# A decode attention kernel: where TensorE's loop lies in its code blocks, and how the second pair's values are loaded

## The chip, the cores and the metric

One core of a Trainium2 chip runs the whole kernel. The metric is the device time of one execution in microseconds; the time of the kernel before is the median of three runs.

## The reference

Attention for one new token: 32 query heads, 8 key/value heads (4 queries share one), 65,536 keys of 128 numbers, all bfloat16.

```
B, Hq, Hkv, Sq, Sk, D = 1, 32, 8, 1, 65536, 128
k = jnp.repeat(k, rep, axis=1); v = jnp.repeat(v, rep, axis=1)     # rep = 4
scores = jnp.einsum("bhqd,bhkd->bhqk", q, k) * D ** -0.5
p = softmax(scores, axis=-1)
return jnp.einsum("bhqk,bhkd->bhqd", p, v)
```

K and V are 134 MB each and every byte is used once, so 268 MB have to come in from memory.

## The kernel before

**Units, pairs, rounds.** The keys of a head are cut into 4 units of 128 x 128 keys; two units make a *pair*, and a *round* works on one pair. There are 16 pairs (`NR`), two for each head. A pair is 256 tiles of 128 keys, 8.39 MB of K and 8.39 MB of V. Tiles 0 to 159 (`A`) go to the first unit of an even pair and the other 96 (`C`) to the second; an odd pair is turned round by `C` tiles, so that it can lie in a ring buffer (`row_tile`).

**What each engine does in a round.** TensorE transposes K in groups of 8 tiles (`pe_transposes`, L139), VectorE and ScalarE copy each group out of PSUM (`evict`, L233 and L235), and 8 groups later TensorE multiplies the transposed tiles with the queries (`pe_scores`, L157). The first 20 groups (`GA`) are one run of code for every round; the last 12 stand in two copies, one under `If(i % 2 > 0)` and one under `If(i % 2 < 1)`, since an odd pair lies elsewhere in the K buffer. VectorE and GpSimd find the maximum, ScalarE the exponentials (L403). Then TensorE multiplies the exponentials with V (`pe_values`, L183) in three *stretches* (`stretch`): stretch 1 is tiles 96 to 159, stretch 2 is tiles 160 to 255, stretch 0 is tiles 0 to 95. Stretch 1 comes first in each round. In an even round stretch 0 follows, then stretch 2, by an inner loop of two turns whose code has stretch 2 ahead of stretch 0: the first turn jumps over stretch 2, and the second jumps back to it. An odd round makes the second turn alone, with both.

**Loops in code.** TensorE's 16 rounds are one loop in its code (`Fori` over `NR`), with some 1,750 instructions in its body. Ahead of it stands an `addr_align(256, offset=LOOP_SLOT, ...)`: the instruction that follows is placed `LOOP_SLOT` instructions behind an address that is a multiple of 256 instructions. `max_nops` is how many empty instructions may fill the room before it; beyond that, the room is jumped over.

**Buffers and transfers.** SyncE issues every load of K and V, in order, in one queue. There is one K buffer with 96 tiles to spare and a single V buffer of one pair. A K load waits for `kfree`, which ScalarE or VectorE sets when the first 20 groups of the pair before are transposed. A V load waits for `vfree`, which VectorE sets in `add_values` when TensorE has finished all stretches of the pair before (`pvd`). Pair 0 is loaded without a wait, K in three parts and V whole. Pairs 2 to 13 go through `load_both`: K whole and V whole. The last two pairs are split into parts again, so that TensorE can start on what has landed.

Pair 1 is loaded by lines of its own. When TensorE ends stretch 1 of round 0 it sets `vmid`; SyncE waits for that and loads the middle of V, tiles 96 to 159, before `vfree`. Behind `vfree` it loads tiles 160 to 255, then 0 to 95, each with a semaphore of its own (`vrdy[0]`, `vrdy[1]`, `vpiece[0]`), for which the stretches of round 1 wait one by one.

Of the kernel before, what the change touches and what calls it, by code (L numbers as in the profile page):

```python
# [13 lines left out]
T = 128  # L14
C = 96
A = 2 * T - C
# [9 lines left out]

V_PIECES = (62, 22, 9, 3)

LOOP_SLOT = 0


def on_act(j):
# [9 lines left out]
def take(e, sem, n=1):  # L42

    e.wait_ge(sem, n)
    e.sem_inc(sem, -n)  # L45


def bass_standalone__gqa_softmax__decode_kernel(nc, q, k, v, out):
# [14 lines left out]
    def row_tile(odd, x):  # L63
        return (x + C) % (2 * T) if odd else x
# [9 lines left out]
    def sem(name):  # L74
        return S(nc.semaphore(name))
# [40 lines left out]
    krdy = [sem(f"krdy{i}") for i in range(len(K_PARTS))]  # L116
    vrdy = [sem(f"vrdy{i}") for i in range(2)]
    vpiece = [sem(f"vpiece{i}") for i in range(len(V_PIECES))]
    kfree, vfree, vmid = sem("kfree"), sem("vfree"), sem("vmid")
    trd, tra, evd, eva = sem("trd"), sem("tra"), sem("evd"), sem("eva")  # L120
    qkd, qrdy, pvd = sem("qkd"), sem("qrdy"), sem("pvd")
    cm, cma, ng, exd, sx, lrd, lra = (sem(n) for n in ("cm", "cma", "ng", "exd", "sx", "lrd", "lra"))
# [41 lines left out]
    def pe_keys(pe, i):  # L164
        for j in range(GA + LAG):
            if j < GA:
                pe_transposes(pe, j, C + j * TB)
            if j >= LAG:
                pe_scores(pe, j - LAG)
        with pe.If(i % 2 > 0):  # L170
            for j in range(GA, G):
                pe_transposes(pe, j, j * TB - A)
        with pe.If(i % 2 < 1):
            for j in range(GA, G):
                pe_transposes(pe, j, C + j * TB)
        for j in range(GA, G):
            pe_scores(pe, j)

    def stretch(pe, q):
        a, b = ((0, C), (C, A), (A, 2 * T))[q]  # L180
        starts = [sum(V_PIECES[:n]) for n in range(len(V_PIECES))] if q == 0 else []
        for r in range(a, b):
            ins = pe.matmul(vsum[q], lhsT=vbuf[:, r * D:(r + 1) * D], rhs=pts[:, r * R:(r + 1) * R],  # L183
                            start=r == a, stop=r == b - 1)
            if r in starts:
                ins.wait_op(vpiece[starts.index(r)], 16, "sem-ge")
        return ins

    def pe_values(pe, i):

        take(pe, vrdy[0], 16)
        take(pe, exd)
        stretch(pe, 1).then_inc(vmid, 1)


        with pe.Fori(i % 2, 2) as s:
            with pe.If(s > 0):
                take(pe, vrdy[1], 16)  # L200
                take(pe, exd)
                stretch(pe, 2).then_inc(pvd, 1)
            with pe.If((i + s) % 2 < 1):
                take(pe, exd)
                stretch(pe, 0).then_inc(pvd, 1)

    def pe_last(pe):
        ins = pe.transpose(fin[0:R, 0:P], acc, identf[:, :])  # L208
        ins.wait_op(t_acc, 1, "sem-ge")
        ins.then_inc(s_fin, 1)  # L210

    def tensor_engine(pe):
        pe.wait_ge(q_sem, 16)
        pe.wait_ge(t_id, 1)
        pe.transpose(trb[0][:, 0:HR], qsb[:, :], ident[0:HR, 0:HR]).then_inc(s_x, 1)
        pe.wait_ge(t_qT, 1)
        pe.addr_align(256, offset=LOOP_SLOT, max_nops=16)
        with pe.Fori(0, NR) as i:
            pe_keys(pe, i)
            pe_values(pe, i)  # L220
        pe_last(pe)
# [221 lines left out]
    def pairs(x):  # L443

        return x.rearrange("h (c p t) d -> (h c) p (t d)", c=HALVES, p=P)

    def sync_engine(e):
        kp, vp = pairs(kf), pairs(vf)

        def cols(a, b):  # L450
            return slice(a * D, b * D)

        def load_k(i, odd, split=(0,)):

            for n, f in enumerate(split):
                last = (split + (len(K_PARTS),))[n + 1]
                a, b = K_PARTS[f], (K_PARTS + (2 * T,))[last]
                r = row_tile(odd, a) if b - a < 2 * T else 0
                t = r if odd else C + r
                e.dma_start(kbuf[:, cols(t, t + b - a)], kp[i][:, cols(r, r + b - a)]).then_inc(krdy[f], 16)  # L460
                for x in range(f + 1, last):
                    e.sem_inc(krdy[x], 16)

        def load_v(i, ready, a, b):
            e.dma_start(vbuf[:, cols(a, b)], vp[i][:, cols(a, b)]).then_inc(ready, 16)

        def load_both(i, odd):
            take(e, kfree)
            load_k(i, odd)
            take(e, vfree)  # L470
            load_v(i, vrdy[0], 0, 2 * T)
            e.sem_inc(vrdy[1], 16)

        load_k(0, 0, (0, 1, 2))
        load_v(0, vrdy[0], 0, 2 * T)

        for sm in [vrdy[1]] + vpiece:
            e.sem_inc(sm, 16)

        take(e, kfree)  # L480
        load_k(1, 1)
        e.wait_ge(vmid, 1)
        load_v(1, vrdy[0], C, A)
        take(e, vfree)
        e.sem_inc(vpiece[0], -16)
        load_v(1, vrdy[1], A, 2 * T)
        load_v(1, vpiece[0], 0, C)
        with e.Fori(1, H - 1) as h:
            load_both(2 * h, 0)
            load_both(2 * h + 1, 1)  # L490
        i = NR - 2
        take(e, kfree)
        load_k(i, 0, (0, 2))
        take(e, vfree)
        load_v(i, vrdy[0], 0, A)
        load_v(i, vrdy[1], A, 2 * T)
        i = NR - 1
        take(e, kfree)
        load_k(i, 1, (0, 1, 2))
        take(e, vfree)  # L500
        for sm in vpiece:
            e.sem_inc(sm, -16)
        load_v(i, vrdy[0], C, 2 * T)
        e.sem_inc(vrdy[1], 16)
        r = 0
        for n, sm in zip(V_PIECES, vpiece):
            load_v(i, sm, r, r + n)
            r += n
        ins = e.dma_start(of[HR - R:HR, :], olast[:, :])
        ins.wait_op(t_last, 1, "sem-ge")  # L510
        ins.then_inc(o_sem, 16)

    with nc.Block() as block:
        block.tensor(tensor_engine)
        block.vector(vector_engine)
        block.scalar(scalar_engine)
        block.gpsimd(gpsimd_engine)
        block.sync(sync_engine)
# [30 lines left out]
```

## Time and profile before

| | |
|---|---|
| median of three runs | 628.77 us (628.72 to 628.85) |
| the profiled execution: its time, its span | 628.62 us, 627.1 us |
| TensorE: multiplies busy, weight loads busy | 490.4 us (78%), 485.9 us (77%) |
| VectorE, ScalarE, GpSimd busy | 284.5 us (45%), 235.4 us (38%), 16.5 us (3%) |
| read from memory | 268.44 MB, 428 GB/s over the span |
| mean granted clock of TensorE | 0.769 |

The span is the time from the first to the last instruction of the profiled execution; 1.5 us of its time lie around it. TensorE's busy time counts pipelined instructions from end to end and follows the granted clock, so it is not a measure of how close it is to its limit. "Queue q1" in the profile is the queue in which SyncE's loads stand; q8 and q14 bring in code. A time to landing is counted from the issue of a transfer to the moment its semaphore is set, and so holds the time for which it stood behind others.

### The profile page before, as it was taken

What the parts mean: (1) busy time and instruction counts of PE and PEld (TensorE: products, weight loads), DVE (VectorE), ACT (ScalarE), POOL (GpSimd) and SP (SyncE); (2) the same over time, 40 slices, a digit from 0 to 9 for tenths busy, and PEclk for the clock granted to TensorE, in tenths of its full rate; (3) what the DMA queues carried; (4) which work ended last, traced back from release to release, by engine and by line L of the source; (5) the groups of instructions that cost most, each with busy time, mean ns of one, the idle gap of its engine ahead of it and who ended that gap; (6) DMA issues with size and microseconds to landing.
All of it is one profiled execution on the core that took longest, in us unless ns stands there. A gap on an engine that the chain in (4) does not pass through costs nothing. (4 is left out here: it accounts for less than half of the span.)

```text
span 627.1 us, 26947 instructions
## 1 busy us (share of the span) xinstructions
PE 490.4 (78%) x12290; PEld 485.9 (77%) x12290; DVE 284.5 (45%) x667; ACT 235.4 (38%) x466; POOL 16.5 (3%) x49
## 2 busy tenths in 40 slices
PE   4664995949959497696976949779595896999887
PEld 3664995949959497696976949779495896989887
DVE  4340553615536164351644516345172452747364
ACT  2240442504425053251533605335052351535343
POOL 0000000000000000000000000000000000000000
PEclk9875886958869597685977959779596785969696
DMA  9999999999999999999999999999999999999997
GB/s 375 430 450 403 442 450 435 435 435 431 422 443 426 435 435 426 439 431 431 435 431 439 431 439 431 435 435 435 435 435 435 435 435 431 412 432 426 432 438 306
DMA packets 6443, 268.59 MB, mean 428 GB/s; under 512 B 802, under 2 KB 930, under 8 KB 1186
## 3 DMA queue, kind: packets, MB, share of 16 engines
q1 hardware_dynamic: 6344, 268.44, 99.2%
q8 instruction: 7, 0.11, 0.1%
q10 hardware_dynamic: 90, 0.02, 0.0%
q14 instruction: 2, 0.02, 0.0%
HBM read 268.44 MB, written 0.01 MB: 428 GB/s over the span
## 5 line engine op out<-in xcount | busy, mean ns | idle before, releaser
L139 PE MATMUL trb<-ident,kbuf 128*128 128x128 bf16 x4096 | 303.4, 237 | 107.4 <-PEq L45 101.7
L139 PEld LDWEIGHTS trb<-ident,kbuf 128*128 128x128 bf16 x4096 | 271.1, 107 | 109.1 <-issue 108.8
L233 ACT ACTIVATE ktb<-trb 128x1024 bf16<-128x1024 bf16 x176 | 180.2, 1024 | 349.9 <-PE trb L139 343.5
L235 DVE COPY ktb<-trb 128x1024 bf16<-128x1024 bf16 x336 | 221.8, 689 | 170.2 <-PE trb L139 167.2
L157 PE MATMUL qkb<-qcur,ktb 128*128 128x4 bf16 x4096 | 132.3, 164 | 1.0 <-issue 1.0
L157 PEld LDWEIGHTS qkb<-qcur,ktb 128*128 128x128 bf16 x4096 | 124.5, 96 | 1.1 <-issue 1.1
L183 PE MATMUL pvb<-pts,vbuf 128*128 128x4 bf16 x2560 | 71.6, 165 | 13.8 <-PEq L45 9.9
L183 PEld LDWEIGHTS pvb<-pts,vbuf 128*128 128x128 bf16 x2560 | 69.8, 101 | 15.6 <-issue 15.2
L403 ACT ACTIVATE pts<-qkb,negm 128x160 bf16<-128x160 f32 (+1 forms) x128 | 52.0, 548 | 0.0
L183 PE MATMUL qkb<-pts,vbuf 128*128 128x4 bf16 x1536 | 43.4, 166 | 7.7 <-PEq L45 7.7
L270 DVE TENSOR_REDUCE cmax<-qkb 128x4 f32<-128x640 f32 (+1 forms) x32 | 22.1, 692 | 59.2 <-DVEq L45 59.2
L183 PEld LDWEIGHTS qkb<-pts,vbuf 128*128 128x128 bf16 x1536 | 42.4, 104 | 8.3 <-issue 8.2
L403 ACT ACTIVATION_READ_ACCUMULATOR pts<-qkb,negm 128x1 f32 x128 | 34.1, 267 | 0.0
L439 POOL PARTITION_ALL_REDUCE cmaxa<-cmax x32 | 12.1, 377 | 576.3 <-POOLq L45 576.3
L320 DVE COPY acc<-qkb 128x4 f32<-128x4 f32 x8 | 1.3, 162 | 41.2 <-DVEq L45 41.2
L397 ACT ACTIVATE alpha<-dm 128x4 f32<-128x4 f32 x32 | 6.4, 201 | 32.4 <-ACTq L45 32.4
L298 DVE TENSOR_TENSOR lp<-lp,alpha 128x4 f32<-128x4 f32 x24 | 3.9, 163 | 26.9 <-DVEq L45 26.9
L309 DVE TENSOR_TENSOR acc<-acc,pvb 128x4 f32<-128x4 f32 x32 | 5.1, 158 | 20.9 <-DVEq L45 20.0
L287 DVE TENSOR_TENSOR m<-m,cmaxa 128x4 f32<-128x4 f32 x24 | 3.8, 160 | 8.8 <-DVEq L45 8.8
L306 DVE TENSOR_TENSOR acc<-acc,alpha 128x4 f32<-128x4 f32 x24 | 3.9, 162 | 4.2 <-DVEq L45 3.7
L299 DVE TENSOR_TENSOR lp<-lp,rsum 128x4 f32<-128x4 f32 x24 | 3.9, 162 | 0.8
L288 DVE TENSOR_TENSOR dm<-m 128x4 f32<-128x4 f32 x24 | 3.9, 162 | 0.8
(42 smaller groups left out, 30.2 us busy)
## 6 DMA issues: line engine op xcount, KB each, us to landing
kbuf<-in_k_dram SPq DMA_DIRECT2D x5, 3072.0 KB, 24.6
vbuf<-in_v_dram SPq DMA_DIRECT2D x2, 5120.0 KB, 23.5
vbuf<-in_v_dram SPq DMA_DIRECT2D x3, 3072.0 KB, 19.9
kbuf<-in_k_dram SPq DMA_DIRECT2D x1, 5120.0 KB, 17.7
kbuf<-in_k_dram SPq DMA_DIRECT2D x2, 2048.0 KB, 12.7
vbuf<-in_v_dram SPq DMA_DIRECT2D x1, 2048.0 KB, 17.8
vbuf<-in_v_dram SPq DMA_DIRECT2D x1, 1984.0 KB, 31.3
vbuf<-in_v_dram SPq DMA_DIRECT2D x1, 704.0 KB, 32.6
```

Source lines behind the costliest of these rows:

```text
L139: ins = pe.transpose(trb[j % NTB][:, i * P:(i + 1) * P], kbuf[:, t * D:(t + 1) * D], ident[:, :])
L157: ins = pe.matmul(bank[:, t * R:(t + 1) * R], lhsT=ktb[:, off:off + P], rhs=qcur[:, :], start=True, stop=True)
L183: ins = pe.matmul(vsum[q], lhsT=vbuf[:, r * D:(r + 1) * D], rhs=pts[:, r * R:(r + 1) * R], start=r == a, stop=r == b - 1)
L233: ins = e.activation(dst, trb[j % NTB][:, :], AF.Copy).then_inc(eva, 1)
L235: ins = e.tensor_copy(dst, trb[j % NTB][:, :]).then_inc(evd, 1)
L270: e.tensor_reduce(cmax[:, :], qkb[part][:, 0:n * R].rearrange("p (t g) -> p g t", g=R), AX.X, ALU.max).then_inc(cm, 1)
L288: lambda: e.tensor_tensor(dm[u % 2][:, :], mo[:, :], mn[:, :], ALU.subtract),
L298: chain(e, lambda: e.tensor_tensor(lp[:, :], lp[:, :], alpha[u % 2][:, :], ALU.mult), lambda: e.tensor_tensor(lp[:, :], lp[:, :], rsum[u % ...
L309: return lambda: e.tensor_tensor(acc, acc, vsum[q], ALU.add)
L397: e.activation(alpha[u % 2][:, :], dm[u % 2][:, :], AF.Exp, scale=scale)
L403: ins = e.activation(pv[:, g, r:r + n], sv[:, g, 0:n], AF.Exp, bias=negm[b][:, g:g + 1], scale=scale, accum_out=rsum[b][:, g:g + 1])
L439: e.partition_all_reduce(cmaxa[:, :], cmax[:, :], P, bass.bass_isa.ReduceOp.max).then_inc(cma, 1)
```

## The change

The loop of TensorE begins 33 instructions behind a multiple of 256 rather than on one, and up to 64 empty instructions may stand ahead of it. The mark `vmid` is gone from TensorE's stretch 1. Pair 1 is loaded as pairs 2 to 13 are: all of K behind `kfree`, then all of V in one load behind `vfree`; the semaphores of the other stretches are then set without a load, as `load_both` does. The instructions of the loop's body are the same in kind, number and order.

```diff
-LOOP_SLOT = 0
+LOOP_SLOT = 33
 ...
-    kfree, vfree, vmid = sem("kfree"), sem("vfree"), sem("vmid")
+    kfree, vfree = sem("kfree"), sem("vfree")
 ...
     def pe_values(pe, i):
         take(pe, vrdy[0], 16)
         take(pe, exd)
-        stretch(pe, 1).then_inc(vmid, 1)
+        stretch(pe, 1)
 ...
         pe.wait_ge(t_qT, 1)
-        pe.addr_align(256, offset=LOOP_SLOT, max_nops=16)
+        pe.addr_align(256, offset=LOOP_SLOT, max_nops=64)
         with pe.Fori(0, NR) as i:
 ...
         for sm in [vrdy[1]] + vpiece:
             e.sem_inc(sm, 16)
-
-        take(e, kfree)
-        load_k(1, 1)
-        e.wait_ge(vmid, 1)
-        load_v(1, vrdy[0], C, A)
-        take(e, vfree)
-        e.sem_inc(vpiece[0], -16)
-        load_v(1, vrdy[1], A, 2 * T)
-        load_v(1, vpiece[0], 0, C)
+        load_both(1, 1)
         with e.Fori(1, H - 1) as h:
             load_both(2 * h, 0)
             load_both(2 * h + 1, 1)
```

`load_both(i, odd)` is `take(e, kfree)`, `load_k(i, odd)`, `take(e, vfree)`, `load_v(i, vrdy[0], 0, 2 * T)`, `e.sem_inc(vrdy[1], 16)`.

## The prediction

> **What bounds the kernel now.** I read the page first, for the share of the DMA engines, then the issues of the K and V loads in order of time with their times to landing, then TensorE's own order of time in the first 63 us.
>
> ```profile
> span 627.1 us, 26947 instructions
> DMA  9999999999999999999999999999999999999997
> q1 hardware_dynamic: 6344, 268.44, 99.2%
> q8 instruction: 7, 0.11, 0.1%
> ```
>
> The queue that moves K and V (q1) fills the 16 DMA engines from end to end, so the kernel is as long as its transfers plus every moment at which they have nothing to do. Next, SyncE's issues in order of time (start us, us, then what), and the end of the run:
>
> ```profile
> 0.74 1.36 SPq L460 DMA_DIRECT2D kbuf<-in_k_dram  x3
> 2.14 0.65 SPq L465 DMA_DIRECT2D vbuf<-in_v_dram  x1
> 26.07 0.33 SPq L460 DMA_DIRECT2D kbuf<-in_k_dram  x1
> 49.85 13.00 SPq L465 DMA_DIRECT2D vbuf<-in_v_dram  x3
> 62.04 0.80 SPq L465 DMA_DIRECT2D vbuf<-in_v_dram  x2
> 76.92 0.35 SPq L460 DMA_DIRECT2D kbuf<-in_k_dram  x1
> L465 SPq DMA_DIRECT2D vbuf<-in_v_dram x23: 327/333/647, 2.1 to 592.1; - x23
> vbuf<-in_v_dram SPq DMA_DIRECT2D x1, 96.0 KB, 32.5
> 622.01 2.89 PE qkb L183 x96
> ```
>
> The fifth row is the last two of the fourth row's three, asked for alone. The last transfer is issued at 592.1 and lands 32.5 us on, at 624.6; TensorE's last stretch ends at 624.9 (622.01 + 2.89) and the span at 627.1. So what the transfers lose anywhere is added to the end. Now the landings of the loads around the change, taken by asking for the issues of short windows (last number: us from issue to landing): the first part of K, V of pair 0, K of pair 1, the middle of V of pair 1, and the last of its three loads.
>
> ```profile
> kbuf<-in_k_dram SPq DMA_DIRECT2D x1, 2048.0 KB, 7.2
> vbuf<-in_v_dram SPq DMA_DIRECT2D x1, 41.3
> kbuf<-in_k_dram SPq DMA_DIRECT2D x1, 36.7
> vbuf<-in_v_dram SPq DMA_DIRECT2D x1, 2048.0 KB, 17.8
> vbuf<-in_v_dram SPq DMA_DIRECT2D x1, 3072.0 KB, 19.9
> ```
>
> V of pair 0 lands at 2.14 + 41.3 = 43.44, K of pair 1 at 26.07 + 36.7 = 62.77: 19.33 us for 8.39 MB, 434 GB/s, which is the engines' pace. The middle of V lands at 49.85 + 17.8 = 67.65, 4.88 us later, where 2.10 MB at that pace take 4.83: no gap, as it had stood in the queue since 49.85. The last of the three, issued at about 62.5, lands at 82.4. So V of pair 1 took 19.63 us in three loads, 0.3 more than one whole load.
>
> **Why the middle stood ready.** TensorE's rows of the first two rounds (start us, us, what, idle before it):
>
> ```profile
> 8.11 6.20 PE L139 MATMUL trb<-ident,kbuf 128*128 128x128 bf16 x64 [2.93 <-PEq L45]
> 16.95 1.01 PE L139 MATMUL trb<-ident,kbuf 128*128 128x128 bf16 x8 [2.63 <-PEq L45]
> 18.01 1.01 PE L139 MATMUL trb<-ident,kbuf 128*128 128x128 bf16 x8
> 19.07 1.01 PE L139 MATMUL trb<-ident,kbuf 128*128 128x128 bf16 x8
> 20.14 0.61 PE L139 MATMUL trb<-ident,kbuf 128*128 128x128 bf16 x8
> 20.79 0.61 PE L139 MATMUL trb<-ident,kbuf 128*128 128x128 bf16 x8
> 25.76 0.27 PE L157 MATMUL qkb<-qcur,ktb 128*128 128x4 bf16 x5
> 27.03 1.83 PE L157 MATMUL qkb<-qcur,ktb 128*128 128x4 bf16 x67 [1.00 <-issue]
> 34.17 6.68 PE L139 MATMUL trb<-ident,kbuf 128*128 128x128 bf16 x91 [5.31 <-issue]
> 41.16 0.44 PE L139 MATMUL trb<-ident,kbuf 128*128 128x128 bf16 x5 [0.30 <-issue]
> 43.92 0.80 PE L183 MATMUL pvb<-pts,vbuf 128*128 128x4 bf16 x25
> 48.64 1.18 PE L183 MATMUL pvb<-pts,vbuf 128*128 128x4 bf16 x39 [3.91 <-issue]
> 56.06 2.70 PE L183 MATMUL qkb<-pts,vbuf 128*128 128x4 bf16 x96 [6.24 <-PEq L45]
> 59.03 2.70 PE L183 MATMUL pvb<-pts,vbuf 128*128 128x4 bf16 x96 [0.27 <-PEq L45]
> 86.54 4.44 PE L183 MATMUL pvb<-pts,vbuf 128*128 128x4 bf16 x160 [0.40 <-PEq L45]
> ```
>
> In round 0 TensorE stops in the middle of runs of equal instructions, waiting for nothing that the profile shows ("issue"), and it never stops so again. Counting a matmul as two instructions (weight load and multiply) and waits, moves and branches as one, the stop at 25.76+0.27 comes after 253 matmuls and 6 others: 512. The stop after 91 transposes is at 1024, that after 25 value matmuls at 1280, and the jump that ends at 56.06 enters the block from 1536 on. With the loop's head at slot 0 these are multiples of 256, and 0.11 MB in 7 instruction packets is 16 KB each, 256 instructions of 64 bytes. So the stops are TensorE's code coming in for the first time, one block at a time: 27.03, 34.17, 41.16, 48.64, 56.06, steps of 7.0 to 7.5 us. Each step begins when the block before it is entered. The code competes with K and V for the DMA engines, and so it is slow. Round 0's values end at 61.73 for this reason alone, V's buffer is free then, and SyncE issues the rest of V at 62.04, 0.73 us before K of pair 1 has landed. The middle, free since 49.82 (48.64 + 1.18), covers the start of the rest.
>
> **The change, part by part.** *One load for V of pair 1.* It waits for the end of round 0's values, and only K of pair 1 is in the queue ahead of it. What a load costs when it is issued to an empty queue is seen once: the first part of K took 7.2 us where its bytes take 4.83, so 2.37 us from issue until it counts as streaming. With TensorE unchanged: issue 62.04 + 2.37 + 19.33 = 83.74 for its landing, against 82.4: +1.3 us.
>
> The engines don't all finish K at once, however. These are the packets in the windows 60.0 to 60.5, 60.5 to 61.0, 61.5 to 62.0 and 62.0 to 62.5; the ones under 512 B are the 16 engines' end marks of that load:
>
> ```profile
> DMA packets 6, 0.05 MB, mean 98 GB/s; under 512 B 3, under 2 KB 3, under 8 KB 3
> DMA packets 11, 0.10 MB, mean 197 GB/s; under 512 B 5, under 2 KB 5, under 8 KB 5
> DMA packets 14, 0.18 MB, mean 360 GB/s; under 512 B 3, under 2 KB 3, under 8 KB 3
> DMA packets 15, 0.16 MB, mean 328 GB/s; under 512 B 5, under 2 KB 5, under 8 KB 5
> ```
>
> Eight engines end near 60.6, eight near 62.1, 61.3 on the mean. If only the late half sets the end, the price is the +1.3 above. If the early half's idle time counts as well, it is some 0.8 us (62.1 - 61.3) more: +2.1. I hold to the first, because each load's landing is that of its latest engine, and keep the second for the range.
>
> One rule of the Trainium skill speaks against the change too: DMA: Bandwidth & Descriptors, in its fit of a DMA's time, gives about 2.0 us fixed per DMA plus the bytes at 436 GB/s. By it the landing would be 62.04 + 2.0 + 19.24 = 83.3, or +0.9; the row of the first part of K says 2.37, and I use the row.
>
> *The loop's head at slot 33.* Every block boundary comes 33 instructions earlier in the code, 16 matmuls. The second block is entered in the run of groups of 8 transposes and 8 scores, which follow each other by 1.06 us (18.01 to 19.07) or 0.65 (20.14 to 20.79): one group earlier, 0.65 to 1.06 us, take 0.85. What follows is the same chain of four more blocks at 7.0 to 7.5 us each, so stretch 0 would begin near 55.2 and the values end near 60.9. This holds if a request made earlier is served earlier. An engine works through 64 KB packets of 2.4 us (64 KB at 434/16 GB/s), so a request 0.85 us earlier may gain nothing, or one whole packet: 0 to 2.4.
>
> Within round 0 the stops move: the transposes of the last group before 26 us come behind the stop, so K of pair 1 is issued up to 1.5 us later than 26.07, hidden by V of pair 0 until 43.44. The stop of 41.16 comes after 75 transposes rather than 91 and leaves 21 behind it, about 1.6 us (0.61 for each 8) in place of 0.44; the next stop (3.91 before) takes that up. The padding ahead of the loop is at most 64 instructions. The trace has none; the nearest row is TensorE's waits, 51 ns each:
>
> ```profile
> L45 PEldq EVENT_SEMAPHORE  x176: 51/51/51, 8.0 to 621.7; - x176
> ```
>
> That is 3.3 us at most, of which 2.93 hide in the wait for K's first part at 8.11 and the rest in the 2.63 at 16.95.
>
> *The mark for SyncE and its wait.* They are gone, and only the issue at 49.85 hung on them. In round 1 the values now wait for the whole load, near 83.1: 3.4 us before they begin at 86.54. K of pair 2 is issued at 76.92, well ahead of that, so no later gap opens.
>
> *Sum.* +1.3 less 0.85 is +0.5 (to +1.3 if the early engines count); I take +0.7. From the profiled run's 628.62 (1.5 outside the span) 629.3; from the median of 628.77, **629.5**. If the values end 1.6 us earlier or more, nothing goes dry, and the 0.3 of the split is gained. So this case reaches from -0.3 to +1.25, 628.5 to 630.0.
>
> **The rivals.** *No head start, and the early engines count* (slower): the blocks arrive when they did, because the packet ahead of the request is the same. Then the price is +1.3 to +2.1: 630.1 to 630.9. It decides once the values end later than about 61.7. For it: the packets' 2.4 us; a slot that isn't put where it is said gives the same. 0.22.
>
> *The loop's tail falls into an eighth block* (slower). Its last branch is the 1752nd instruction after slot 0; at 33 it stands at 1785, six slots short of 1791. Any padding at the branch targets there pushes the end of the inner loop over the edge. Stretch 0 then ends at 58.8 and TensorE waits for that block before it can go back for stretch 2. Its packet of before is this, in the window 60.6 to 60.7:
>
> ```profile
> q8 instruction: 1, 0.02, 62.4%
> ```
>
> The block would come near 63.2 (56.06 + 7.2), the values end at 66.2, V lands near 88.2: +5.8, or +5.0 with the head start: 633.8 to 634.6. Against it: the count leaves room. 0.16.
>
> *Code that no longer stays.* The seven packets in 16 rounds show that seven blocks stay on hand. With an eighth and the block fetched behind it, they might not: eight steps of 7.2 us are 57.6 us for each round, against 38.7 of transfers, so about 285 us more, above 900. The Trainium skill (Runtime: NRT & Kernel Launch, Instruction fetch mechanics) gives TensorE 128 KiB, eight blocks, which fits the trace as far as it goes; the same section speaks of a two-block window, which the seven packets contradict. By the eight, this rival needs the ninth block to be fetched. 0.04.
>
> *Faster by over 0.2%.* The first load lost 2.37 us to its start and part of that might be TensorE's code; losing that and the 0.3 could give -1.5, 627.3. The first K load's issue doesn't wait for TensorE. 0.04.
>
> **How the numbers follow.** About 0.2%, 1.26 us, is what a measurement of this kernel can tell from no change. The forecast has 0.54, all within it; slower is 0.22 + 0.16 + 0.04 = 0.42, faster 0.04. The range goes from 628.3 to 634.3: the forecast with 0.2 to spare below, the first rival and most of the second.
>
> **What would show it.** Right: one V issue between 60.5 and 62.1, its landing between 82.2 and 84, stops of TensorE after 237 matmuls, 75 transposes and 9 value matmuls, and later loads all shifted alike. Wrong: an instruction packet that TensorE waits for between stretch 0 and stretch 2, more than 7 or 8 of them in the run, or transfers that catch up again after pair 1.

## The result, and the profile after

The changed kernel takes 630.24 us (median of 18 runs, 628.69 to 631.55), the kernel before 628.71 (18 runs, 628.57 to 628.94): a ratio of 1.0024, 95% interval 1.0018 to 1.0031. It is slower by 1.5 us, and it scatters over 2.9 us where the kernel before scatters over 0.4. The profiled execution is the longest of the 18, 631.55: 2.65 us of it lie outside its span, where most runs have 1.3 to 1.6. Its span of 628.9 us is an ordinary one; the 18 spans run from 626.9 to 629.9, and their median is 628.8.

The page of the kernel after, its head and its DMA queues:

```profile
span 628.9 us, 26945 instructions
q1 hardware_dynamic: 6056, 268.44, 99.0%
q8 instruction: 7, 0.11, 0.1%
```

The span is 1.8 us longer (627.1 before), within the span the code still comes in by seven packets, and the bytes are the same. SyncE's issues around the change (start us, us, what), and from issues of short windows the times to landing of K of pair 1, V of pair 1 and K of pair 2:

```profile
24.87 0.33 SPq L460 DMA_DIRECT2D kbuf<-in_k_dram  x1
59.70 0.33 SPq L465 DMA_DIRECT2D vbuf<-in_v_dram  x1
76.33 0.34 SPq L460 DMA_DIRECT2D kbuf<-in_k_dram  x1
kbuf<-in_k_dram SPq DMA_DIRECT2D x1, 38.1
vbuf<-in_v_dram SPq DMA_DIRECT2D x1, 24.4
kbuf<-in_k_dram SPq DMA_DIRECT2D x1, 27.1
```

K of pair 1 lands at 24.87 + 38.1 = 62.97, V of pair 1 at 59.70 + 24.4 = 84.10, K of pair 2 at 103.43. So V of pair 1 takes 21.13 us where a load takes 19.33, and that is where the time goes: K of pair 1 lands only 0.2 us later than before, K of pair 2 is back at 19.33, and from there to the end every landing is 1.7 to 1.9 us later than before. The first part of the last V, before and after:

```profile
590.27 2.23 SPq L465 DMA_DIRECT2D vbuf<-in_v_dram  x5
vbuf<-in_v_dram SPq DMA_DIRECT2D x1, 5120.0 KB, 26.9
592.19 2.23 SPq L465 DMA_DIRECT2D vbuf<-in_v_dram  x5
vbuf<-in_v_dram SPq DMA_DIRECT2D x1, 5120.0 KB, 26.8
```

It lands at 617.17 before and at 618.99 after. Nothing is made up later.

What was not foreseen is that V was issued at 59.70, 3.3 us *ahead* of K's end. TensorE's order of time says why it was so early:

```profile
16.80 0.61 PE L139 MATMUL trb<-ident,kbuf 128*128 128x128 bf16 x8 [3.06 <-PEq L45]
31.86 6.23 PE L139 MATMUL trb<-ident,kbuf 128*128 128x128 bf16 x75 [5.36 <-issue]
38.87 1.35 PE L139 MATMUL trb<-ident,kbuf 128*128 128x128 bf16 x21 [0.78 <-issue]
43.65 0.38 PE L183 MATMUL pvb<-pts,vbuf 128*128 128x4 bf16 x9 [1.05 <-PEq L45]
46.42 1.63 PE L183 MATMUL pvb<-pts,vbuf 128*128 128x4 bf16 x55 [2.39 <-issue]
53.78 2.70 PE L183 MATMUL qkb<-pts,vbuf 128*128 128x4 bf16 x96 [5.73 <-PEq L45]
56.75 2.70 PE L183 MATMUL pvb<-pts,vbuf 128*128 128x4 bf16 x96 [0.27 <-PEq L45]
```

The stops come after 75 transposes and 9 value matmuls, as the slot count says. Each block of code comes 2.2 to 2.3 us earlier than before (31.86 for 34.17, 53.78 for 56.06), and round 0's values end at 59.45 in place of 61.73. Not all of this need come from the slot: the groups of 8 transposes from 16.8 us on take 0.61 us here, where the first three of the profile before took 1.01. The granted clock of that stretch, the second of the page's 40 slices, is 0.9 here and was 0.8 there, so TensorE would have been earlier at this point at slot 0 too.

Where the 1.8 us go, the packets show. First K's end: the windows 60.5 to 61.0 and 62.0 to 62.5, then shorter windows, 60.8 to 60.9, 63.0 to 63.1 and 63.85 to 63.89. A q1 row holds packets, MB, and the share of 16 engines in the window, by the whole time of the packets that start in it:

```profile
DMA packets 15, 0.46 MB, mean 918 GB/s; under 512 B 8, under 2 KB 8, under 8 KB 8
DMA packets 13, 0.39 MB, mean 786 GB/s; under 512 B 7, under 2 KB 7, under 8 KB 7
q1 hardware_dynamic: 9, 0.26, 767.6%
q1 hardware_dynamic: 1, 0.07, 235.3%
q1 hardware_dynamic: 1, 0.07, 445.0%
```

Eight of the first row's packets and seven of the second's are under 512 B, K's end marks; the rest are V's first packets. The early half of the engines goes on at once, 1.1 to 1.3 us after V's issue, but with slow packets: 767.6% of 1.6 engine-microseconds, over four packets of data (nine less five marks), is 3.07 us each, where 2.42 is usual. The late half goes on at 62.0 to 62.5 without a gap, but for two engines. Their end marks of K stand at 61.7 and 62.3 with no packet of V behind them; the two packets that are missing there start at 63.05 and 63.88, 3.3 and 4.2 us after the issue. So these two engines stand idle in between, for 0.8 to 2.2 us. Then V's end, the windows from 81.0, 81.5, 82.0, 82.5 and 83.5 on:

```profile
DMA packets 13, 0.46 MB, mean 918 GB/s; under 512 B 6, under 2 KB 6, under 8 KB 6
DMA packets 11, 0.39 MB, mean 786 GB/s; under 512 B 5, under 2 KB 5, under 8 KB 5
DMA packets 4, 0.13 MB, mean 262 GB/s; under 512 B 2, under 2 KB 2, under 8 KB 2
DMA packets 2, 0.07 MB, mean 131 GB/s; under 512 B 1, under 2 KB 1, under 8 KB 1
DMA packets 11, 0.59 MB, mean 1180 GB/s; under 512 B 2, under 2 KB 2, under 8 KB 2
```

Eleven engines are done by 82.0; two come at 83.6 to 83.8. These are the two that started late: their first packets take 3.77 and 2.85 us (235.3% of 1.6, 445.0% of 0.64), and seven more of 2.42 bring them to 83.8 and 83.7. A load lands with its last engine. As the delay stays to the end of the run, it seems that no other engine takes over a late one's share.

### The profile page after: what moved, and what is told of

The parts are those of the page before. It is cut to its first block, busy times and chain, and to the rows that moved or that the text cites. A ratio compares the mean times of both kernels' runs of the same rounds, so it can differ in the third digit from the quotient of the medians.

```text
span 628.9 us, 26945 instructions
## 1 busy us (share of the span) xinstructions
PE 482.0 (77%) x12290; PEld 477.4 (76%) x12290; DVE 283.7 (45%) x667; ACT 235.4 (37%) x466; POOL 16.4 (3%) x49
## 5 line engine op out<-in xcount | busy, mean ns | idle before, releaser
L139 PE MATMUL trb<-ident,kbuf 128*128 128x128 bf16 x4096 | 294.8, 233 | 121.0 <-PEq L45 114.8
L139 PEld LDWEIGHTS trb<-ident,kbuf 128*128 128x128 bf16 x4096 | 262.8, 105 | 122.8 <-issue 120.2
L270 DVE TENSOR_REDUCE cmax<-qkb 128x4 f32<-128x640 f32 (+1 forms) x32 | 22.1, 691 | 58.3 <-DVEq L45 58.3
L403 ACT ACTIVATION_READ_ACCUMULATOR pts<-qkb,negm 128x1 f32 x128 | 34.2, 267 | 0.0
## 6 DMA issues: line engine op xcount, KB each, us to landing
kbuf<-in_k_dram SPq DMA_DIRECT2D x5, 3072.0 KB, 24.4
```

The costliest lines, as they stand in the source:

```text
L139: ins = pe.transpose(trb[j % NTB][:, i * P:(i + 1) * P], kbuf[:, t * D:(t + 1) * D], ident[:, :])
L270: e.tensor_reduce(cmax[:, :], qkb[part][:, 0:n * R].rearrange("p (t g) -> p g t", g=R), AX.X, ALU.max).then_inc(cm, 1)
L403: ins = e.activation(pv[:, g, r:r + n], sv[:, g, 0:n], AF.Exp, bias=negm[b][:, g:g + 1], scale=scale, accum_out=rsum[b][:, g:g + 1])
```

## The experiments

Theory A: V of pair 1 is issued with too little lead over the end of what is queued. Its rivals are the shape of the load (B) and the slot itself (C). The first four kernels cross slot, shape and lead. All are set beside the kernel before on the same chip (628.61 to 628.68).

**slot33_split**: slot 33 alone, the loads as before.

```diff
-LOOP_SLOT = 0
+LOOP_SLOT = 33
-        pe.addr_align(256, offset=LOOP_SLOT, max_nops=16)
+        pe.addr_align(256, offset=LOOP_SLOT, max_nops=64)
```

> The loop's head at slot 33, pair 1's V in three loads with the middle ahead of the buffer's release, as before. Theory A (the loss of 1.8 us in V of pair 1 comes from its late issue, too few us ahead of K's end): the middle covers it, so the time of before, 628.7 within 0.3, and V of pair 1 takes 19.3 to 19.7 us after K of pair 1. Theory B (the shape: one load of 64 KB rows at this place is slow): 628.7 too. Theory C (the slot itself costs something): 630.2, as the changed kernel. The release of V's buffer should come near 59.7 by all three, if the slot moves the code blocks.

628.74 us, ratio 1.0008 (0.9999 to 1.0017). The span is 627.1 to 627.3 in ten of eleven runs, as before; C falls, as far as the span goes. The rest of V is issued at 59.71, so the early release is here too. Four runs take 629.6 to 630.2, 2.3 to 2.6 us outside the span in place of 1.5; that is followed up below.

**slot0_one_load**: the other half of the change alone.

```diff
 LOOP_SLOT = 0
-        ... (pair 1's lines with vmid)
+        load_both(1, 1)
```

> The loop's head at slot 0, pair 1's V in one load behind the release. Theory A: the release comes near 62.0, 0.7 us ahead of K's end, so the loss is larger than 1.8: 2 to 3 us, 630.8 to 631.7, and with less scatter than the changed kernel has. Theory B: the same as the changed kernel, 630.2. Theory C: the time of before, 628.7.

630.58 us (630.49 to 630.66), ratio 1.0030 (1.0019 to 1.0041). The loss of A, without scatter, but just under the 630.8 to 631.7 that I gave, and hardly more than at slot 33. SyncE's issue, its time to landing, and the packets in 62.2 to 63.1, 63.1 to 63.2 and 66.2 to 66.3:

```profile
62.20 0.33 SPq L465 DMA_DIRECT2D vbuf<-in_v_dram  x1
vbuf<-in_v_dram SPq DMA_DIRECT2D x1, 21.9
DMA packets 2, 0.00 MB, mean 0 GB/s; under 512 B 2, under 2 KB 2, under 8 KB 2
q1 hardware_dynamic: 5, 0.33, 983.0%
q1 hardware_dynamic: 5, 0.33, 756.4%
```

Here the queue does run dry: no packet of V starts before 63.1, 0.9 us after the issue, and the first take 3.15 us (983.0% of 1.6, over 5), the next 2.42. V lands 21.9 us after its issue, 2.57 more than its 19.33; the prediction had 2.37 from the first part of K. The Trainium skill's fit (DMA: Bandwidth & Descriptors, Anatomy of one DMA — SWDGE (gpsimd) path), 2.0 us and the bytes, is given there for DMAs on the path of GpSimd, not of SyncE; by it the landing here would be, as an estimate, 83.4, and it was 84.10.

**slot33_three_late**: the changed kernel, with V in three loads, all behind the release.

```diff
-        load_both(1, 1)
+        take(e, kfree)
+        load_k(1, 1)
+        take(e, vfree)
+        e.sem_inc(vpiece[0], -16)
+        load_v(1, vrdy[0], C, A)
+        load_v(1, vrdy[1], A, 2 * T)
+        load_v(1, vpiece[0], 0, C)
```

> The loop's head at slot 33, pair 1's V in the three loads of before, but all three issued behind the release. Theory A: the issue is as late as in the changed kernel, so about as slow, 629.8 to 630.5. Theory B: the shape of before, so 628.7. Theory C: 630.2.

630.32 us, ratio 1.0030 (1.0020 to 1.0041): B falls. Three smaller loads are as slow as one when they are as late.

**slot33_cover16**: the changed kernel, with 16 of V's 256 tiles ahead of the release.

```diff
-        load_both(1, 1)
+        take(e, kfree)
+        load_k(1, 1)
+        e.wait_ge(vmid, 1)
+        load_v(1, vrdy[0], A - 16, A)
+        take(e, vfree)
+        load_v(1, vrdy[0], 0, A - 16)
+        load_v(1, vrdy[1], A, 2 * T)
```

(Not shown: stretch 1 sets `vmid` again, and `vrdy[0]` counts two loads in every round.)

> The changed kernel with the last 16 tiles of the middle (1.2 us of transfer) loaded ahead of the release, as soon as stretch 1 has ended, and the rest in two loads behind it. Theory A: 1.2 us of cover raises the lead of the rest from 3.3 to 4.5 us; what is left of the loss is 0 to 0.6 us, 628.7 to 629.3. Theory B: two larger loads rather than one, 629 to 630. Theory C: 630.2.

628.75 us, ratio 1.0004 (0.9995 to 1.0013), all spans 627.1 to 627.3: 1.2 us of transfer standing in the queue take the whole 1.7 us away.

**slot0_cover16** and **slot0_cover32**: the same at slot 0, with 16 and with 32 tiles (`A - 32`).

> The head at slot 0 with 16 tiles (1.2 us) of V of pair 1 loaded ahead of the release and the rest behind it. The release comes near 62.0, so the rest is issued some 2 us ahead of the end of what is queued, against 3.3 in the changed kernel. Theory A1 (what counts is the lead over the end of the queue): a loss of 0.4 to 1.8 us, 629.1 to 630.5. Theory A2 (any load still queued keeps the engines going, however small): no loss, 628.7. If 4 us after the issue were needed for every engine, 630 or more.

> As the one with 16 tiles at slot 0, but with 32 tiles (2.4 us): the rest is issued about 3.2 us ahead of the queue's end, the same lead as the changed kernel has. Theory A1: a loss as in the changed kernel, 0 to 1.8 us with scatter, 628.7 to 630.5. Theory A2: 628.7.

16 tiles: 630.45 us, ratio 1.0022 (1.0012 to 1.0032); three spans of 627.2 or 627.3, seven from 628.6 to 629.6. 32 tiles: 628.77, ratio 1.0010 (1.0000 to 1.0019); eight spans of 627.0 to 627.3, three from 628.5 to 629.1. A2 falls: a small load in the queue isn't enough. The spans come in two kinds, and the two profiled runs are one of each. The rest's issues in them, 16 tiles first, then 32:

```profile
62.11 0.80 SPq L465 DMA_DIRECT2D vbuf<-in_v_dram  x2
59.96 0.80 SPq L465 DMA_DIRECT2D vbuf<-in_v_dram  x2
```

So at slot 0 the release comes at 62.1 or at 59.9 as well. Put together, the profiled executions give this (lead: landing of what is queued less the issue of the rest; loss: the span over 627.1 to 627.3):

| profiled execution | release used at | queue's end | lead | loss |
|---|---|---|---|---|
| slot0_one_load | 62.20 | 62.95 | 0.8 | 1.9 |
| slot0_cover16 | 62.11 | 64.04 | 1.9 | 2.1 |
| slot33_three_late | 59.89 | 62.79 | 2.9 | 1.7 |
| the changed kernel | 59.70 | 62.97 | 3.3 | 1.7 |
| slot16_one_load (below) | 59.69 | 62.96 | 3.3 | 1.9 |
| slot33_cover16 | 59.85 | 64.07 | 4.2 | 0 |
| slot33_k1_small_end (below) | 57.71 | 63.0 | 5.3 | 0 |
| slot0_cover32 | 59.96 | 65.33 | 5.4 | 0 |
| kernel before | 62.04 | 67.65 | 5.6 | 0 |

In these executions it is nearly all or nothing, and the step lies between 3.3 and 4.2 us. Each line is one execution, though: among the 18 spans of the changed kernel are also 626.9, 627.6 and three from 628.2 to 628.4, and no trace of those is there to tell their lead. The packets ahead differ as well: 64 KB in the changed kernel, 4 KB in the 16 tiles of slot33_cover16. In the kernel before, the shortest lead of a whole load is 4.8 us (K issued at 270.99, the V ahead of it landed at 275.76), and nothing is lost there. So behind packets of 64 KB the step is only known to lie between 3.3 and 4.8 us.

**slot64_split**: the loads of before, the head at slot 64, so that the loop reaches into an eighth block.

```diff
-LOOP_SLOT = 0
+LOOP_SLOT = 64
-        pe.addr_align(256, offset=LOOP_SLOT, max_nops=16)
+        pe.addr_align(256, offset=LOOP_SLOT, max_nops=64)
```

> The loads of before and the head at slot 64, so that the loop's last branch stands at slot 1816 and its tail in an eighth block of code. If eight blocks and the one fetched behind them all stay: TensorE waits once more in round 0, ahead of stretch 2, until about 61 to 63; the release comes near 64 to 66, still ahead of the end of the queued middle at 67.6, but by 2 to 3 us only; 628.7 to 630. If they don't stay: instruction packets in every round, TensorE's rounds of up to 57 us, 700 to 920.

710.97 us (707.24 to 712.55), ratio 1.1317 (1.1301 to 1.1332). The page's instruction queue, and TensorE in rounds 0 and 1:

```profile
q8 instruction: 79, 1.29, 0.7%
60.47 0.43 PE L183 MATMUL qkb<-pts,vbuf 128*128 128x4 bf16 x11 [4.08 <-issue]
92.68 2.50 PE L157 MATMUL qkb<-qcur,ktb 128*128 128x4 bf16 x90 [2.00 <-issue]
99.94 0.30 PE L157 MATMUL qkb<-qcur,ktb 128*128 128x4 bf16 x6 [4.76 <-issue]
107.17 1.25 PE L183 MATMUL pvb<-pts,vbuf 128*128 128x4 bf16 x41 [3.52 <-issue]
```

79 packets in place of 7, and stops inside runs of equal matmuls in round 1, which no kernel above has. In round 0 the eighth block arrives at 60.47, with 11 matmuls of stretch 0 still to do, so the block's edge lies where the second rival had counted it.

**slot16_one_load**: the changed kernel with the head at slot 16 (`LOOP_SLOT = 16`).

> The changed kernel with the head at slot 16 in place of 33. If the arrival of the code goes by whole packets of 64 KB (2.4 us), the release comes either near 59.7 or near 62.1 and nothing between; if it goes by the 8 matmuls of head start, near 61.6. The time is then 630.2 with scatter (59.7) or 630.6 without (62.1). If the scatter of the time outside the span (1.5 to 2.6 us at slot 33, 1.5 at slot 0) belongs to the loop's end lying at the edge of its block, it is 1.5 here.

630.00 us, ratio 1.0023 (1.0014 to 1.0032). The release is used at 59.69, the early value, with half of the head start: the code's arrival goes by whole packets. The time outside the span is 1.3 to 1.4 us in all eleven runs.

**slot24_split**: the kernel before with the head at slot 24 (`LOOP_SLOT = 24`, and `max_nops=64` as at slot 33).

> The kernel before with the head at slot 24, so that its last instructions end some 12 slots ahead of the block's edge; at slot 33 they end 2 or 3 ahead of it. If the 0.8 to 1.1 us that some runs at slot 33 show outside the span belong to the edge, the time outside is 1.3 to 1.6 us in every run and the median 628.6 to 628.8. If any head other than 0 brings them, some runs come out near 629.6 again.

628.65 us (628.54 to 628.73), ratio 1.0000 (0.9990 to 1.0009); 1.44 to 1.55 us outside the span in every run. At slot 33 four kernels show over 1.9 us outside in 2 to 5 of 8 or 11 runs, and the changed kernel in 4 of 18. So this belongs to slot 33, whose code ends, by my count, 2 to 3 instructions ahead of a block's edge, and not to every slot other than 0. The traces reach a little beyond the span and show something there. This is the changed kernel in 630.7 to 630.8, 1.8 us behind the end of its span:

```profile
q8 instruction: 1, 0.02, 65.3%
```

It is an eighth packet of code, one block. The three traces at slot 33 with 2.1 to 2.7 us outside the span (the changed kernel, slot33_cover16, slot33_k1_small_end) have one, 1.4 to 1.9 us behind the span's end; the two with 1.5 (slot33_split, slot33_three_late) and all those at slots 0, 16 and 24 have none. So the longer ends go with a block fetched behind the program's last instructions. That the end waits for it, and why it comes in some runs only, isn't shown.

**slot33_k1_small_end** and **slot0_k1_small_end**: the one load of V kept, K of pair 1 in two loads, the second of 24 KB rows, to see whether the lead is counted in packets or in microseconds.

```diff
-        load_both(1, 1)
+        take(e, kfree)
+        load_k(1, 1, (0, 2))
+        take(e, vfree)
+        load_v(1, vrdy[0], 0, 2 * T)
+        e.sem_inc(vrdy[1], 16)
```

> The changed kernel, but K of pair 1 in two loads, so that what stands in the queue when V of pair 1 is issued near 59.7 are packets of 24 KB (0.9 us) in place of 64 KB (2.4 us). Issue and queue's end as in the changed kernel, lead 3.3 us. Theory P (a new load reaches a busy engine behind two packets that it has already taken up): the wait falls from 3.3 to 4.4 us to under 2, no engine runs dry, 628.5 to 628.9. Theory L (it takes a fixed 4 us, whatever the packets): the loss stays, 629.9 to 630.5.

> The same with the head at slot 0, where V of pair 1 is issued near 62.1, some 0.8 us ahead of the end of K, if TensorE's code comes in as before. Theory P: the start of about 1 us on an idle engine and the slow first packet stay, so a loss of 1.3 to 2 us, 630.0 to 630.6, less in a run in which the release comes near 59.8. Theory L: 630.4 to 630.7.

629.39 us (ratio 1.0012, 1.0003 to 1.0021) and 630.81 (1.0040, 1.0027 to 1.0054). The times don't tell the theories apart: the smaller packets let the code in faster as well, and V is issued at 57.71 and 57.73 in the profiled executions, a lead of 5 us and no loss. In others the loss is there: spans of 628.1 to 628.4 in four of eleven, and of 629.3 to 630.3 in four of five. But the code's own wait is a sign for theory P: from entering a block to the packet of the next it is 4.5 to 5 us before, behind packets of 64 KB, and 2.7 to 3.7 us in these two runs while the first part of K, in packets of 40 KB, comes in (51.78 to 54.43, for one).

## Why the prediction was right or wrong

**The sign and the place were right, the path to them was not.** 630.24 lies in the range, and just over the 0.2% that I had called "the same". The loss is in V of pair 1 alone and stays to the end, as forecast; but the sum had two wrong terms that partly cancel, so the sign is in part luck: with the head start that was measured, the same sum gives a gain. The forecast's own band, 628.5 to 630.0, was missed, and the 0.54 on "the same" just failed.

**The term of the slot was too small.** I took 0.85 us of head start, and named 2.4 as the other end. It was 2.3 (31.86 for 34.17), about a whole packet of 64 KB (2.42), and half of the shift in slots (16) brings as much. It isn't sure either. Taking the stop at 31.8 in place of 34.2 as the sign of the early code, which comes before K of pair 1 is moved at all, two of five profiled executions at slot 0 have it (slot0_cover32 and slot0_k1_small_end), and all eight at slots 16 to 64. With the same loads, slot33_cover16 keeps the span of before in eleven runs of eleven and slot0_cover16 in three of ten. So the slot makes the early code far more likely, but isn't alone in setting it.

**The step that failed** is "if the values end 1.6 us earlier or more, nothing goes dry, and the 0.3 of the split is gained". They ended 2.3 us earlier, and by that step the time would have been 628.5. The price of 2.37 us for a load issued to an empty queue was nearly right where the queue is empty (2.57 at slot 0, and 2.4 to 2.8 in slot64_split, where TensorE is so late that six whole loads of V meet an empty queue and take 21.7 to 22.1 us); the mistake was to subtract the lead from it, as if it were worked off microsecond by microsecond. A lead of 3.3 us costs what a lead of 0.8 costs, one of 4.2 nothing. And the 0.3 us that I put down to the split didn't show: slot33_cover16 and the kernel before have the same span.

**The rivals.** "No head start, and the early engines count" has the size (1.3 to 2.1, measured 1.5), but by the wrong mechanism: the head start was there. At slot 0 it came out as it was described, at 1.9. The loop did not enter the eighth block at slot 33: seven packets within the span, and 0.27 us ahead of stretch 2. That was right, and slot64_split shows that the place of the edge was counted rightly. Code that doesn't stay was real where I doubted it: with the loop in eight blocks it is fetched again, 72 packets more in 15 rounds, for 82 us in place of the 285 I gave. I had priced every block of every round at the full 7.2 us; it was under five blocks a round. As far as it goes, this agrees with the eight blocks that the Trainium skill gives TensorE (Runtime: NRT & Kernel Launch, Instruction fetch mechanics): eight of the loop and the one behind it are too many.

**Right by its own steps:** the stops after 75 transposes and 9 value matmuls, one V issue, K of pair 2 issued well ahead (76.33 for a V that lands at 84.10), no catching up. The stop after 237 matmuls didn't show, as the block was there by then.

**What stays open:** why a lead of 3.3 us loses nearly as much as none. The packets show where: two engines of sixteen that take up V only 3.3 and 4.2 us after its issue, and slow packets on the others. A fixed wait of 4 us for every engine is ruled out, as eight take V up after 1.1 to 1.3 us. Two packets of 2.4 us ahead of anything new would fit the code's waits of 4.5 to 5 us, but not these two engines, which were done with K at 61.7 and 62.3 and then idle. Why it is those two isn't known.

## What to carry to other kernels

Where the transfers are the bound, issue a load while the queue still holds a few microseconds of work (here, behind packets of 64 KB, a lead of 3.3 us lost and one of 4.8 didn't), not merely before it is empty; read the lead as the landing of the load ahead less the issue, for every load, and cover the short ones with a piece that is free sooner, long enough to bring the lead up (1.2 us of V did it at slot 33, but not on the late release at slot 0). A loop's code comes in behind the data the first time through: count its instructions in blocks of 256, and see which stop falls on the path to the next release. Keep the loop, and if it can be the program's last instructions too, clear of the edge of the last block that stays.

## What the runs showed of the hardware that was not expected

- A load that follows on too short a lead pays in its first packets (3.07 to 3.15 us for 64 KB in place of 2.42) and in single engines that start late; two of sixteen set the end of the load, some 1.7 us behind the eleven that were done by 82.0, and the run is 1.8 us longer.
- One block of code too many costs 82 us: seven blocks for 16 rounds take 7 instruction packets, eight take 79.
- A program whose last instructions lie 2 to 3 slots ahead of a block's edge shows 0.5 to 1.4 us more outside the span in about a third of its runs; the three such runs with a trace fetch one more block of code, 1.4 to 1.9 us behind the span's end.
